# Matmuls of zeros, whose results nobody reads, in four idle stretches of TensorE at the start of an attention, Fourier mixing and MLP kernel

## The chip, the cores and the metric

The kernel runs on one core of one Trainium2 chip. The metric is the device time of one execution in microseconds (us); lower is better. A core has five engines that each work through their own list of instructions in order: PE (TensorE, the matmuls; its weight loads are listed apart as PEld), DVE (VectorE), ACT (ScalarE), POOL (GpSimd) and SP (SyncE, which here issues the DMAs). They meet only at semaphores.

## The reference, cut to what matters

Shapes: batch 8, 8 heads, 576 tokens, head width 64, 32 memory slots, model width 512, hidden width 2048.

```python
a = softmax(phi, over the 32 slots)                       # pooling weights, (8, 8, 576, 32)
k_m, v_m = einsum('bhsm,bhsd->bhmd', a, k), einsum(same, a, v)
attn_out = softmax(q @ k_m.T / 8) @ v_m
x = attn_out with heads side by side                      # (8, 576, 512)
u = x + real(fft(fft(x, axis=1), axis=2))
un = (u - mean(u)) / sqrt(var(u) + 1e-6)                  # over the last axis
out = u + relu(un @ w_ch1) @ w_ch2                        # (512 -> 2048 -> 512)
```

The two weights arrive as 64 bit floating point numbers.

## The kernel before, in words

The tokens are worked off in 36 tiles of 128. A generator called background makes tiles of u for one batch after another; the main loop takes two finished tiles at a time (a chunk, 18 in all), normalises them and runs the two MLP matmuls over eight slices of the hidden width, while background makes the tiles that come next.

The change lies in the head, everything before the first chunk's MLP. For batch 0 it runs so, and the names are those of the profile:

- SP issues the loads in a fixed list: phi (phs), four pairs of heads (k, v and q of a pair in rawt, stg and twice in w2s), the Fourier tables ct and vt, a mask mk (in small), and the first three slices of both weights (w1t, w2s, stg).
- pooling_weights: PE transposes phi (pf and pl, L292), DVE takes the maxima (L293 to L297), ACT the exponentials (L301, L302) and the scaling (L311), PE transposes back (pt_e, L314, and pl, L317), and DVE and ACT copy the result to et (L315, L318).
- pair_memory, for the four pairs: k and v are pooled by f32 matmuls with 64 moving columns (pm, issued at L255; each f32 matmul leaves two records, so 80 in all), and DVE masks what comes out (L346, L347; these need mk).
- pair_scores, for the four pairs: q times the pooled k (psc, also L255, 48 records of the same shape), then the softmax over the slots, mostly on DVE (L440 to L480) with the exponential on ACT (L450).
- values and spectrum: the Fourier transforms by matmul (pv L521, pa L540 and L548) and transposes (pt_vbd, pt_attnT, L246).
- mix_m, mix_x and add_mix: pp_t and px_t on PE, then u in uring on DVE (L603, L617).
- norm_chunk(0): statistics on DVE (L631 to L640), a power on POOL (L641), un on DVE (L642); then PE transposes un (pt_unT, L657) and ACT copies it to unring (L658).
- Then the first chunk's MLP in f32, slice by slice (ph L675, po L692), with the conversion of each weight slice from 64 to 32 bits: ACT L771 and L793, DVE L773, L774 and L784 (and L779 with POOL L782 for some slices). The sum of squares of a slice goes through PE as as_sq (L214). The conversion of the first slice of w1 needs nothing but its load, and stands early on DVE.

From the second chunk on the matmuls are f16 (ph L255 and po L728), which is the long steady part.

The order of each engine's list isn't the order of the code. The program is given to a scheduler that places every instruction by its own forecast of when it can run, and the lists that it makes are then fixed. A forecast that changes in one place can so exchange neighbours on other engines too.

PSUM has 8 banks here: four of pool psg (tag g), two of ps1, two of ps2 (tag o, which the MLP's sums po use later). uring is a ring of eight tiles of 128x512 f32, and its slot 7 is first written by the eighth tile of u.

Of the kernel before, what the change touches and what calls it, by code (L numbers as in the profile page):

```python
# [10 lines left out]
F32 = mybir.dt.float32  # L11
F16 = mybir.dt.float16
# [26 lines left out]
NU = 8  # L39
NHS = 7  # L40
STEPS = 2
NX = 2
GATE1 = [[]] + [["un1", "uh0"]] * 7
GATE2 = [["un1", "uh0"]] * 8
# [87 lines left out]
def kernel(  # L132
# [42 lines left out]
    ident = small[:, 768:832].bitcast(F16)  # L175
    make_identity(nc, ident)
    identf = const.tile([P, P], F32, name="identf")
    make_identity(nc, identf)
# [5 lines left out]
    unring = const.tile([P, 2, 2, CH, NK, P], F16, name="unring")  # L184
    uring = const.tile([P, NU, DM], F32, name="uring")
    hring = const.tile([P, NW, 2, 4, P], F16, name="hring")
# [29 lines left out]

    qi = [0]

    def norm_scale(dst_s, dst_i, sq, n, expo, key):
# [12 lines left out]
        )  # L232
        nc.vector.reciprocal(out=dst_s, in_=dst_i)

    def transpose(dst, src, on_pe, key):
# [13 lines left out]
    def groups():  # L249
# [3 lines left out]
        def mm(out, lhsT, rhs, start, stop):  # L253
            with tc.issue_after(last[0].ins) if start and last[0] is not None else nullcontext():
                m = nc.tensor.matmul(out, lhsT=lhsT, rhs=rhs, start=start, stop=stop)  # L255
            if stop:
                last[0] = m

# [24 lines left out]
    def pooling_weights(b):  # L283
# [4 lines left out]
        for g in range(2):  # L288
            pf.append(psg.tile([P, 512], F32, tag="g", name=f"pf_{b}_{g}"))
            for t in range(NST):  # L290
                dst = pf[g][:, t * P : (t + 1) * P] if t < 4 else pl[:, g * P : (g + 1) * P]
                nc.tensor.transpose(dst, phs[:, t, 2 * g : 2 * g + 2].rearrange("p g c -> p (g c)"), identf)  # L292
            nc.vector.tensor_reduce(out=mx[:, g : g + 1], in_=pf[g], axis=AX.X, op=ALU.max)  # L293
        rest = pl[:, : 2 * P].rearrange("p (g s) -> p g s", g=2)[:, :, : S - 4 * P]
        nc.vector.tensor_reduce(out=mx[:, 2:4], in_=rest, axis=AX.X, op=ALU.max)
        nc.vector.tensor_tensor(out=mx[:, 0:2], in0=mx[:, 0:2], in1=mx[:, 2:4], op=ALU.max)
        nc.vector.tensor_scalar(out=mx[:, 0:2], in0=mx[:, 0:2], scalar1=-1.0, scalar2=None, op0=ALU.mult)  # L297
        su = tiny("su", 4, 2)
        for g in range(2):
# [8 lines left out]
        for g in range(2):  # L308
            r = su[:, 2 + g : 3 + g]
            if b < NX:  # L310
# [5 lines left out]
                half_t = pl[0 : S - 4 * P, (2 + g) * P : (3 + g) * P]  # L316
                nc.tensor.transpose(half_t, pht[:, g, 4 * P :], identf)  # L317
                nc.scalar.copy(out=et32[0 : S - 4 * P, g, 4], in_=half_t)  # L318
# [595 lines left out]

    load_phi(0)
    first = [load_pair(0, 0)]
    nc.sync.dma_start(out=mk, in_=mk_d)
# [33 lines left out]
    while made < 2:  # L951
        made, room = next(bg)
    unTs = {0: norm_chunk(0)}
    hs = {c: [] for c in range(n_chunks)}
# [107 lines left out]
```

## Time and profile before

| what | us |
| --- | --- |
| median of 3 runs | 996.77 (996.4 to 997.15) |
| the profiled execution, its own time | 996.51 |
| the profiled execution, from its first to its last instruction (span) | 994.6 |
| PE busy in the span | 955.8 |
| DVE busy in the span | 568.1 |
| PE busy in the first 50 us | 34.1 |
| PE's longest idle stretches in the first 70 us, by the timeline of PE | 0 to 4.26, 7.40 to 13.43, 44.2 to 48.7, 59.97 to 65.26 |

Some 1.9 us of the execution lie around the span. A row of the timeline gives the start, the duration, the engine, the line, the operation and the tiles (what is written, then what is read), the shape and the number of instructions merged into it; in brackets stands how long the engine had been idle and what ended that. A row of the table of stretches gives, for each engine, its busy time and its number of instructions, then the granted clock of TensorE as a share of full speed, the share of the DMA engines' time and their rate. A row of the chain of waits gives a start, a time, and the work that the end of the program hung on in that time.

### The profile page before, as it was taken

How to read it: one execution, taken by the hardware profiler on the slowest of the kernel's cores; microseconds unless marked ns; L12 is line 12 of the kernel's file. 1: busy time of each engine (PE TensorE's matmuls, PEld its weight loads, DVE VectorE, ACT ScalarE, POOL GpSimd, SP SyncE). 2: the span in 40 equal slices, each digit the busy share in tenths (PEclk: the TensorE clock that was granted, in tenths of full speed). 3: DMA queues.
4: the chain of work that ended last, by engine and by line, in shares of the span. 5: the costliest groups of instructions: out<-in, count | busy, mean ns of one | idle time of the engine just before them, and what ended most of it. 6: DMA issues, size and time to landing. Idle time of an engine off the chain costs nothing.

```text
span 994.6 us, 18638 instructions
## 1 busy us (share of the span) xinstructions
PE 955.8 (96%) x7644; PEld 685.8 (69%) x7644; DVE 568.1 (57%) x1287; ACT 456.3 (46%) x913; POOL 228.0 (23%) x249
## 2 busy tenths in 40 slices
PE   5769999899999999999999999999999999999998
PEld 5756678666677777767767767777777777766664
DVE  1689967867655575657532576657745676311111
ACT  2265557586535563655431555456545543411100
POOL 1122235235221241233120032113311241300000
PEclk9979999999999999999999999999999999999999
DMA  9706545064222641384210643164213411210000
GB/s 351 270 1 253 184 152 154 2 138 117 64 43 59 136 98 41 56 153 103 58 22 22 117 120 61 48 119 121 68 43 62 101 19 35 44 39 4 22 22 22
DMA packets 115957, 88.06 MB, mean 89 GB/s; under 512 B 100384, under 2 KB 100384, under 8 KB 113824
## 3 DMA queue, kind: packets, MB, share of 16 engines
q1 hardware_dynamic: 115872, 86.87, 34.6%
q8 instruction: 60, 0.98, 0.4%
q14 instruction: 25, 0.20, 0.1%
HBM read 58.15 MB, written 9.44 MB: 68 GB/s over the span
## 4 chain that ended last, share of the span: by engine, by line
PE 84%; DVE 9%; ACT 2%; DMA 2%; issue 1%; SPq 0%; POOL 0%; DVEq 0%; ACTq 0%; POOLq 0%
PE po L728 34%; PE ph L255 33%; PE pm L255 5%; PE pp_t L255 3%; PE psc L255 2%; PE px_t L255 1%; PE pa L548 1%; PE pv L521 1%; PE po L692 1%; DVE w1t L784 1%; DVE uring L617 1%; DVE w2s L774 1%; DMA et<-elt 1%; DMA uring<-in_w 1%; DMA rawt<-in_raw 1%
## 5 line engine op out<-in xcount | busy, mean ns | idle before, releaser
L255 PE MATMUL ph<-unring,w1t 128*128 128x256 f16 x3264 | 390.3, 273 | 2.4 <-DVE scratch L638 1.4
L728 PE MATMUL po<-w2s,hring 128*128 128x512 f16 x1632 | 381.1, 380 | 3.1 <-ACT w2s L838 1.8
L255 PEld LDWEIGHTS <-w1t 128*128 128x128 f16 x3264 | 316.0, 98 | 66.3 <-issue 2.6
L728 PEld LDWEIGHTS <-hring 128*128 128x128 f16 x1632 | 157.6, 98 | 161.5 <-issue 5.6
L719 DVE SCALAR_TENSOR_TENSOR hring<-ph,hring 128x512 f16<-128x512 f32 x136 | 93.3, 686 | 157.4 <-ACT hring L718 156.9
L718 ACT ACTIVATE hring<-ph 128x512 f16<-128x512 f32 x136 | 80.1, 589 | 167.7 <-PE ph L255 167.6
L456 POOL TENSOR_TENSOR aring<-aring,scratch 128x384 f32<-128x384 f32 x28 | 24.7, 882 | 186.6 <-DVE scratch L454 163.5
L641 POOL TENSOR_TENSOR scratch<-scratch,small 128x1 f32<-128x1 f32 x36 | 23.9, 679 | 165.6 <-DVE scratch L640 152.9
L255 PEld LDWEIGHTS <-stg 128*128 128x128 f16 x1152 | 46.1, 98 | 10.3 <-issue 1.7
L373 POOL TENSOR_TENSOR stg<-rawt,stg 128x640 f16<-128x640 f32 x12 | 17.6, 1464 | 122.4 <-ACT rawt L372 122.4
L662 POOL TENSOR_TENSOR ud<-un,ud 128x1024 f16<-128x1024 f32 x17 | 36.7, 2160 | 33.9 <-ACT ud L661 33.8
L255 PE MATMUL pm<-et,stg 128*128 128x64 f16 (+1 forms) x780 | 39.1, 203 | 2.0 <-DMA et<-elt 2.0
L440 DVE TENSOR_REDUCE scratch<-psc 128x12 f32<-128x384 f32 x32 | 17.8, 556 | 39.2 <-PE psc L255 39.1
L255 PE MATMUL pp_t<-vh,at 128*128 128x255 f16 (+3 forms) x288 | 36.7, 273 | 0.0
L603 DVE SCALAR_TENSOR_TENSOR share<-pp_t,scratch,small 128x257 f32<-128x257 f32 (+1 forms) x48 | 21.0, 479 | 26.6 <-ACT small L600 26.5
L740 DVE SCALAR_TENSOR_TENSOR uring<-po,small,uring 128x512 f32<-128x512 f32 x34 | 24.5, 744 | 19.2 <-PE po L728 19.2
L675 PE MATMUL ph<-unring,w1t 128*128 128x256 f32 x128 | 33.5, 409 | 2.0 <-DVE w1t L784 1.5
L475 ACT CAST aeo<-eo 128x384 f16<-128x384 f32 x30 | 15.3, 510 | 43.9 <-DVE eo L472 43.9
L450 ACT ACTIVATE aring<-aring,scratch 128x384 f32<-128x384 f32 x24 | 14.6, 610 | 45.0 <-DVE aring L449 45.0
L617 DVE SCALAR_TENSOR_TENSOR uring<-px_t,scratch,share 128x256 f32<-128x256 f32 (+1 forms) x80 | 33.9, 476 | 0.2
L692 PE MATMUL po<-w2s,hring 128*128 128x512 f32 x64 | 31.5, 621 | 2.4 <-ACT hring L678 2.4
L675 PEld LDWEIGHTS ph<-unring,w1t 128*128 128x128 f32 x128 | 26.0, 207 | 11.1 <-issue 4.6
(226 smaller groups left out, 1271.9 us busy)
## 6 DMA issues: line engine op xcount, KB each, us to landing
rawt<-in_raw SPq DMA_DIRECT2D x15, 640.0 KB, 5.6
stg<-in_raw SPq DMA_DIRECT2D x15, 640.0 KB, 5.1
out<-uring SPq DMA_DIRECT2D x36, 256.0 KB, 2.1
stg<-in_w SPq DMA_DIRECT2D x7, 1024.0 KB, 5.1
rawt<-in_raw SPq DMA_DIRECT2D x15, 384.0 KB, 3.2
stg<-in_raw SPq DMA_DIRECT2D x15, 384.0 KB, 3.2
phs<-in_raw SPq DMA_DIRECT2D x32, 160.0 KB, 5.2
w2s<-in_w SPq DMA_DIRECT2D x4, 1024.0 KB, 9.6
```

Source lines behind the costliest of these rows:

```text
L255: m = nc.tensor.matmul(out, lhsT=lhsT, rhs=rhs, start=start, stop=stop)
L456: eng.tensor_tensor(out=a, in0=a, in1=sm.unsqueeze(2).to_broadcast([P, 12, M]), op=ALU.mult)
L603: nc.vector.scalar_tensor_tensor(out=tm[rows, w * NJ : (w + 1) * NJ], in0=pp[rows, :NJ], scalar=beta[rows], in1=qs[rows], op0=ALU.mult, op ...
L617: nc.vector.scalar_tensor_tensor(out=u[rows, hs], in0=px[rows, hs], scalar=igx[rows], in1=tm[rows, w * NJ + half : w * NJ + half + 256], o ...
L641: nc.gpsimd.tensor_tensor(out=rs, in0=rs, in1=half, op=ALU.pow)
L662: marks[f"ul{c}"] = nc.gpsimd.tensor_tensor(out=ud[:, 1], in0=un, in1=ud[:, 0], op=ALU.subtract)
L675: nc.tensor.matmul(ph, lhsT=w[:, k, f * P : (f + 1) * P], rhs=unTs[0][:, k], start=(k == 0), stop=(k == NK - 1))
L692: nc.tensor.matmul(po[t], lhsT=h[:, f, t], rhs=w[:, f], start=(j == 0 and f == 0), stop=(j == NW - 1 and f == UB - 1),)
L718: nc.scalar.activation(h[:, 0], phv, AF.Relu)
L719: nc.vector.scalar_tensor_tensor(out=h[:, 1], in0=phv, scalar=0.0, in1=h[:, 0], op0=ALU.max, op1=ALU.subtract)
L728: nc.tensor.matmul(po[t], lhsT=hs[j][:, lh, f * 2 + t], rhs=w2s[:, j * UB + f, lw, :], start=(j == 0 and f == 0 and i == 0), stop=(j == NW ...
L740: nc.vector.scalar_tensor_tensor(out=u, in0=po[t], scalar=cout if c else 0.5, in1=u, op0=ALU.mult, op1=ALU.add)
```

## The change

A block of 128x512 f16 zeros is made once, by a memset on DVE, in the memory of uring's slot 7. A new function keep_busy(n) issues n matmuls that read this block both as weights (its first 128 columns) and as moving operand (all 512), and write a PSUM tile of the pool ps2 that nothing reads. Each call is placed behind the last matmul or transpose that had been marked so far. Seven counts stand in a table; four are above zero:

- KEEP[0] = 8, right after the loads of phi, ahead of all other work of PE;
- KEEP[1] = 26, after the first transposes of phi and the maxima, ahead of pt_e;
- KEEP[6] = 3, after the second pt_e, ahead of the first pm;
- KEEP[4] = 22, after px_t of the first two tiles, ahead of pt_unT.

That is 59 matmuls of 128x512 f16. No load and no instruction with a result is added or taken away.

```diff
+KEEP = [8, 26, 0, 0, 22, 0, 3]
...
+    uring = const.tile([P, NU, DM], F32, name="uring")
+    zeros = uring[:, NU - 1].bitcast(F16)[:, :DM]
+    nc.vector.memset(zeros, 0.0)
...
+    def keep_busy(n):
+        pt = ps2.tile([P, 512], F32, tag="o", name=f"keep_{len(kept)}")
+        kept.append(pt)
+        with tc.issue_after(marks["pe"].ins) if "pe" in marks else nullcontext():
+            for _ in range(n):
+                nc.tensor.matmul(pt, lhsT=zeros[:, :P], rhs=zeros, start=True, stop=True)
...
             if stop:
-                last[0] = m
+                last[0] = marks["pe"] = m
...
+        if b == 0:
+            keep_busy(KEEP[1])
         su = tiny("su", 4, 2)
...
-                nc.tensor.transpose(half_t, pht[:, g, 4 * P :], identf)
+                marks["pe"] = nc.tensor.transpose(half_t, pht[:, g, 4 * P :], identf)
+                if b == 0:
+                    keep_busy(KEEP[5 + g])
...
     load_phi(0)
+    keep_busy(KEEP[0])
...
     while made < 2:
         made, room = next(bg)
+    keep_busy(KEEP[4])
     unTs = {0: norm_chunk(0)}
```

What this does to the engines' lists is shown at three places. The first is PE from the second group of phi's transposes to the first pooling matmul. Before:

```order
L292 MATMUL pf_1_135<-identf,phs 128x128 x4
L292 MATMUL pl_127<-identf,phs 128x128
L314 MATMUL pt_e_0_153<-identf,phs 128x128 x4
L317 MATMUL pl_127<-identf,phs 64x128
L314 MATMUL pt_e_1_162<-identf,phs 128x128 x4
L317 MATMUL pl_127<-identf,phs 64x128
L255 MATMUL pm_0_170<-et,rawt 128x64 x10
```

Now (rows of the zeros that only repeat are left out; they read uring and write keep):

```order
L304 MATMUL pf_1_145<-identf,phs 128x128 x4
L304 MATMUL pl_137<-identf,phs 128x128
L245 LDWEIGHTS uring
L245 MATMUL keep_155<-uring 128x512
...
L328 MATMUL pt_e_0_190<-identf,phs 128x128 x4
L331 MATMUL pl_137<-identf,phs 64x128
L328 MATMUL pt_e_1_200<-identf,phs 128x128 x4
L331 MATMUL pl_137<-identf,phs 64x128
L245 LDWEIGHTS uring
L245 MATMUL keep_207<-uring 128x512
...
L267 MATMUL pm_0_212<-et,rawt 128x64 x10
```

Twenty-six pairs stand between the transposes and pt_e, and three between the last pl and pm; the rest of PE's list is as it was down to the last psc. (L245 is the added line; the lines behind it are some 12 to 18 higher than before.)

The second place is DVE between the last maskings of pm and the softmax of the first pairs. Before:

```order
L347 TENSOR_TENSOR vmf<-pm_1_183,small 128x128
L773 TENSOR_SCALAR w1t<-w1t 128x1024
L774 SCALAR_TENSOR_TENSOR w1t<-w1t 128x1024
L784 SCALAR_TENSOR_TENSOR w1t<-w1t 128x1024
L346 TENSOR_TENSOR share<-pm_2_196,small 128x64
L347 TENSOR_TENSOR vmf<-pm_2_196,small 128x128
L346 TENSOR_TENSOR share<-pm_3_209,small 128x64
L347 TENSOR_TENSOR vmf<-pm_3_209,small 128x128
L440 TENSOR_REDUCE scratch<-psc_0_222 128x12
L449 TENSOR_TENSOR aring<-psc_0_222,scratch 128x384
L452 TENSOR_REDUCE scratch<-aring 128x12
```

Now:

```order
L363 TENSOR_TENSOR vmf<-pm_1_225,small 128x128
L362 TENSOR_TENSOR share<-pm_2_238,small 128x64
L363 TENSOR_TENSOR vmf<-pm_2_238,small 128x128
L362 TENSOR_TENSOR share<-pm_3_251,small 128x64
L363 TENSOR_TENSOR vmf<-pm_3_251,small 128x128
L789 TENSOR_SCALAR w1t<-w1t 128x1024
L790 SCALAR_TENSOR_TENSOR w1t<-w1t 128x1024
L456 TENSOR_REDUCE scratch<-psc_0_264 128x12
L800 SCALAR_TENSOR_TENSOR w1t<-w1t 128x1024
L456 TENSOR_REDUCE scratch<-psc_1_288 128x12
L465 TENSOR_TENSOR aring<-psc_0_264,scratch 128x384
```

The three steps that convert the first slice of w1 stood between the second and the third pair's masking; now two of them stand behind the fourth pair's and the third behind the first reduction of the scores. Behind these rows the softmax of the four pairs and the values' steps are interleaved differently, with the same operations. On SP the load of mk and that of the first slice of w1 have exchanged places, so mk now goes first.

The third place is PE ahead of the transposes of the first normalised tiles. Before:

```order
L255 MATMUL px_t_441<-vbdt,attnT 128x128
L255 LDWEIGHTS attnT
L255 MATMUL px_t_452<-vbdt,attnT 128x128
L255 LDWEIGHTS attnT
L657 MATMUL pt_unT_468<-identf,un 128x128 x4
L657 MATMUL pt_unT_479<-identf,un 128x128 x4
```

Now:

```order
L267 LDWEIGHTS attnT
L267 MATMUL px_t_494<-vbdt,attnT 128x128
L245 LDWEIGHTS uring
L245 MATMUL keep_505<-uring 128x512
...
L673 MATMUL pt_unT_533<-identf,un 128x128 x4
L673 MATMUL pt_unT_544<-identf,un 128x128 x4
```

Twenty-two pairs stand between px_t and pt_unT. Behind this place neighbours have changed places here and there up to the end of the first chunk; from the third batch on every list is as it was.

More of the change, by code (lines that the diff above doesn't have):

```diff
@@ L184 @@
     unring = const.tile([P, 2, 2, CH, NK, P], F16, name="unring")
-    uring = const.tile([P, NU, DM], F32, name="uring")
     hring = const.tile([P, NW, 2, 4, P], F16, name="hring")
@@ L217 @@
     qi = [0]
+    kept = []
     def norm_scale(dst_s, dst_i, sq, n, expo, key):
@@ L291, in pooling_weights @@
                 dst = pf[g][:, t * P : (t + 1) * P] if t < 4 else pl[:, g * P : (g + 1) * P]
-                nc.tensor.transpose(dst, phs[:, t, 2 * g : 2 * g + 2].rearrange("p g c -> p (g c)"), identf)
+                marks["pe"] = nc.tensor.transpose(dst, phs[:, t, 2 * g : 2 * g + 2].rearrange("p g c -> p (g c)"), identf)
             nc.vector.tensor_reduce(out=mx[:, g : g + 1], in_=pf[g], axis=AX.X, op=ALU.max)
```

## The prediction

> **What bounds the kernel now.** I began with the page's head and its slices of the span, to see where PE isn't full.
>
> ```profile
> span 994.6 us, 18638 instructions
> PE 955.8 (96%) x7644; PEld 685.8 (69%) x7644; DVE 568.1 (57%) x1287; ACT 456.3 (46%) x913; POOL 228.0 (23%) x249
> PE   5769999899999999999999999999999999999998
> PEclk9979999999999999999999999999999999999999
> ```
>
> PE sets the pace from the third slice on; only the head, the first two slices, has holes. What is won there is kept if the part behind is a plain queue for PE. So I next asked for stretches: the head piece by piece, a piece of the next batch, and the steady part.
>
> ```profile
> 7.40:13.40 6.00, 0.00 (x1) 0.00 (x0) 1.54 (x7) 4.12 (x11) 0.00 (x0) 1.00 1.02 412
> 15.60:43.00 27.40, 27.40 (x130) 27.24 (x128) 12.29 (x32) 5.01 (x9) 1.47 (x2) 1.00 1.01 378
> 48.70:52.30 3.60, 3.58 (x23) 2.04 (x25) 3.60 (x11) 1.48 (x4) 1.77 (x3) 1.00 0.00 0
> 59.90:65.20 5.30, 0.07 (x2) 0.00 (x0) 4.60 (x14) 0.00 (x0) 1.17 (x2) 0.75 0.00 0
> 65.20:72.80 7.60, 7.08 (x22) 6.04 (x23) 6.11 (x10) 6.14 (x7) 1.83 (x1) 0.50 0.00 1
> 72.80:94.10 21.30, 20.83 (x114) 14.67 (x112) 21.30 (x31) 11.96 (x21) 3.32 (x2) 1.00 0.53 205
> 147.80:151.30 3.50, 3.50 (x34) 3.50 (x33) 2.81 (x7) 0.71 (x2) 0.67 (x1) 1.00 0.67 150
> 209.00:995.00 786.00, 780.81 (x6574) 547.39 (x6573) 415.94 (x940) 345.09 (x704) 171.81 (x189) 1.00 0.31 67
> ```
>
> The columns are PE, PEld, DVE, ACT, POOL, then the granted clock and the DMA share. Three limits follow one another: PE alone from 15.6 to 43.0 (27.40 of 27.40 us, DVE under half), DVE alone from 72.8 to 94.1 (21.30 of 21.30), PE from 209 on (780.81 of 786). Zeros in PE's holes (7.4 to 13.4, 59.9 to 65.2) can pay only through the clock, and the clock column seems to leave little: it shows 0.50 from about 62.5 to 72.7 and 1.00 before that. That 1.00 is what I doubted. A column of shares can't say whether a stretch without a record was at full speed; the duration of one shape can. The groups of PE, shapes apart, in the first 60 us and from 128 to 158 us:
>
> ```profile
> L255 PE MATMUL pm<-et,w2s 128*128 128x64 f32 x40 | 8.7, 421 | 0.0
> L255 PE MATMUL pm<-et,stg 128*128 128x64 f32 x40 | 4.8, 275 | 0.0
> ```
>
> After the bar stand busy us, the mean ns of one, and idle us. One shape takes 421 ns in batch 0 and 275 in batch 1. In the chain of waits it is the pace, not only the latency, that differs:
>
> ```profile
> 13.43 1.12 PE pt_e L314 x4
> 15.83 16.96 PE pm L255 x80
> 32.79 5.13 PE psc L255 x24
> 124.54 0.66 PE pt_e L314 x4
> 138.98 1.28 PE psc L255 x12
> 148.92 2.23 PE pm L255 x20
> 233.93 2.16 PE po L728 x10
> ```
>
> pm runs at 16.96/80 = 0.212 us a record in the head and 2.23/20 = 0.1115 later; psc at 5.13/24 = 0.214 against 1.28/12 = 0.107. A factor of 1.9 to 2.0 is a clock at half. And the timeline of PE shows when it ended:
>
> ```profile
> 50.48 0.94 PE L548 MATMUL pa<-ct,aeo 128*128 128x145 f16 x6
> 54.26 0.55 PE L548 MATMUL pa<-ct,aeo 128*128 128x145 f16 x6
> 67.88 6.11 PE L675 MATMUL ph<-unring,w1t 128*128 128x256 f32 x16 [0.46 <-ACT unring L658]
> 80.36 3.67 PE L675 MATMUL ph<-unring,w1t 128*128 128x256 f32 x16
> ```
>
> So I read PE as at half clock from the start to about 52 us, and again to 72.7. It stayed so through 27 us of unbroken work, while wide matmuls raised it soon: f16 around 50 us, and ph in the second dip. The narrow ones are held by their weight loads (27.24 of 27.40 busy): at the half clock 64 columns take 0.212 us and 256 take 6.11/16 = 0.382, four times the columns in 1.8 times the time, so the array streams at most half the time. That is too little to raise the clock. Is it enough to keep it? The stretch 147.8 to 151.3 says so: 34 records, nearly all pm and psc, PEld full, and 1.00 throughout.
>
> **The change part by part.** The price of a zero is 2.16/10 = 0.216 us, since po is f16 of 128x512 too, and by the factor of two 0.43 at half clock.
>
> KEEP[0]: eight at half clock are 3.5 us, in a hole of 4.26; the memset ahead of them is one DVE instruction of 128x256, under 0.7 us by the reduction of twice as many elements at 35.39 below. Cost: between 0 and 0.2 us; I take nothing.
>
> KEEP[1]: the hole it lies in, from the timeline of PE:
>
> ```profile
> 4.26 1.09 PE L292 MATMUL pf<-identf,phs 128*128 128x128 f32 x4 [4.26 <-POOL small L195]
> 6.98 0.42 PE L292 MATMUL pl<-identf,phs 128*128 128x128 f32 x1
> 13.43 1.12 PE L314 MATMUL pt_e<-identf,phs 128*128 128x128 f32 x4 [6.03 <-ACT phs L311]
> ```
>
> 26 zeros take 5.6 us at full clock in 6.03, so they are hidden by ACT's exponentials if the clock is up by about 8.2 us; each us later costs 0.5 us, and a clock that never rises costs 26 x 0.43 - 6.03 = 5.1. In front of 7.4 us PE has then worked for some 6 of 7 us, more than the stretch around 50 us that raised it, so I expect the rise between 4 and 11 us: 0 to 1.4 us late, and if pf and pl come faster, 0.4 early. I take 0. KEEP[6]: three are 0.65 us, while pt_e shortens from 1.12 to 0.66 twice; between ACT's two scalings and the copies of et the two cancel. pm starts where it did.
>
> Then the gain. pm: 80 x (0.212 - 0.1115) = 8.0 us. The first pair's psc: 12 x 0.107 = 1.3. The other three pairs' scores come out faster than DVE takes them, and give nothing more. The first scores are ready 9.3 us earlier, at 26.1 in place of 35.4. Who takes them is DVE, and its order has changed:
>
> ```profile
> 21.06 0.23 DVE L346 TENSOR_TENSOR share<-pm,small 128x64 f32<-128x64 f32 x1 [4.71 <-DMA small<-in_mk]
> 24.63 0.68 DVE L773 TENSOR_SCALAR w1t<-w1t 128x1024 int32<-128x1024 int32 x1
> 25.35 1.23 DVE L774 SCALAR_TENSOR_TENSOR w1t<-w1t 128x1024 int32<-128x1024 int32 x1
> 26.61 1.22 DVE L784 SCALAR_TENSOR_TENSOR w1t<-w1t 128x1024 uint32<-128x1024 uint32 x1
> 35.39 0.56 DVE L440 TENSOR_REDUCE scratch<-psc 128x12 f32<-128x384 f32 x1 [2.14 <-PE psc L255]
> 37.12 0.55 DVE L452 TENSOR_REDUCE scratch<-aring 128x12 f32<-128x384 f32 x1 [0.59 <-ACT aring L450]
> ```
>
> The mask lands by 21 us, before the second pair's pm is over, and its load goes one place earlier: no new wait. The conversion of w1 used to fill a hole of DVE; now there is none. The fourth pm ends at 15.8 + 8.9 = 24.7, its masking at 25.1, the two conversions (0.7 + 1.25) at 27.1: the first reduction is 1.0 us late, and the third conversion puts 1.2 us ahead of the second. Loss 2.2. Against it, other pairs' reductions now stand in the wait of 0.59 for ACT: gain 0.5. From there to un DVE and ACT do the same work, so un comes 9.3 - 2.2 + 0.5 = 7.6 us earlier.
>
> Next come the last matmuls ahead of un, by PE's timeline:
>
> ```profile
> 57.32 1.48 PE L255 MATMUL pp_t<-vh,at 128*128 128x257 f16 x12
> 58.63 1.34 PE L255 MATMUL px_t<-vbdt,attnT 128*128 128x128 f16 x16
> ```
>
> In between PE idles after psc as it did, for want of DVE, and the clock falls again. Whether it is back by pp_t depends on how densely pv and pa come; before, it was back at 52. If it isn't, pp_t and px_t take up to 1.48 + 1.34 us more, and the zeros of KEEP[4] start slow. At full clock 22 are 4.75 us in the 5.3 us hole that DVE's statistics leave; with half of them slow they end 1 us late. I bound this by 0 and +3.7 us and take +0.4. Behind the zeros:
>
> ```profile
> 65.26 1.94 PE L657 MATMUL pt_unT<-identf,un 128*128 128x128 f32 x8 [5.29 <-DVE un L642]
> 67.24 0.59 ACT L658 COPY unring<-pt_unT 128x512 f32<-128x512 f32 x1 [0.21 <-PE pt_unT L657]
> 67.72 1.12 ACT L771 ACTIVATE w2s<-w2s 128x1024 f32<-128x1024 f32 x1
> 72.91 1.13 ACT L803 ACTIVATE w1t<-w1t,small 128x1024 f16<-128x1024 f32 x1
> ```
>
> With the clock kept, pt_unT halves and ACT's second copy comes 0.8 us earlier. ph saves 2.4 us (6.11 to 3.67), but ACT has L771 to L803 to do until 74 us whatever PE does, and DVE is full after that: nothing more.
>
> [...]
>
> Sum: -7.6 - 0.8 + 0.4 = -8.0 us. The profiled execution took 996.51, 0.26 below the median of 996.77, so the forecast is 988.5 against the first and 988.7 against the median. Behind the head DVE's full stretch and then PE's move as a whole.
>
> **The rivals.** First, the clock rises and falls back within pm and psc: a longer unbroken run of narrow matmuls than the 3.5 us that were seen at 1.00. Half way through, 4.7 us of the 9.3 are won, and the conversion again lies partly in DVE's waits: 991.5 to 993.
>
> Second, zeros don't raise the clock: no row shows a matmul of zeros. Then KEEP[1] ends at 7.4 + 11.1 = 18.5 and pt_e starts 5.1 us late, KEEP[6] adds 1.3, and PE's narrow run, still at half clock, sets the scores 6.4 us later; KEEP[4] lies behind real work that raised the clock at 52 and fits. 996.5 + 6.4 = 1002.9. It ends slower only if the clock is still low through pm; a rise by 11 us costs but 1.4. For it: nothing but the missing row. Against it: the engine works through the same instruction.
>
> Third, the 421 ns aren't the clock: the DMA engines are full from 15.6 to 43.0 (1.01), and their writes might slow the weight loads. Then only KEEP[4] pays: 996.5 - 0.8 = 995.7. Against it stand six pa in 0.94 us at 50 us with a DMA share of 0.00 (48.7 to 52.3), and in 0.55 four us later.
>
> Fourth, the gain is made and lost again up to 209 us, by exchanged neighbours or by loads: near 996. The loads for later slices are issued when DVE frees their room and move with it, which speaks against it.
>
> **How the numbers follow.** Forecast 0.75; rivals 0.09, 0.06, 0.05, 0.05. The likeliest case's own range: early by 0.4, no loss in the tail and the two conversions better hidden (-3) give 985.5; 1.4 late at KEEP[1] and 3.7 in the tail give 993.8. Some 0.72 lies in there; with the first rival, up to 994.5, it is 0.8. About 0.2%, 2 us, is what a measurement of this kernel tells from no change. Faster: 0.75 + 0.09 = 0.84. Same: 0.05 + 0.05 = 0.10. Slower: 0.06.
>
> **What would show it.** Right: pm of batch 0 at 275 ns from its first record, pt_e at 0.66 us for four, the first L440's counterpart near 27 us, un near 57.5, no stretch at 0.50 behind pt_unT, and the 786 us from 209 on unchanged. Wrong: pm at 421; pt_e starting at 18 us; DVE's first reduction early but pt_unT not; or a clock that drops within the narrow run.

## The result, and the profile after

The changed kernel took 990.29 us (median of 3 runs, 988.95 to 991.04) against 996.77 (996.4 to 997.15): a ratio of 0.9933, with a 95% interval of 0.991 to 0.9956. It is faster, and the forecast was 988.7. One thing has to be known from the start: executions of the kernel before fall into two groups some 8 us apart (shown below), and the three that the ratio was taken from all lay in the upper one.

The page of the profile after, its head and the slices of PE and of the granted clock:

```profile
span 988.3 us, 18757 instructions
PE 955.3 (97%) x7703; PEld 675.8 (68%) x7703; DVE 566.7 (57%) x1288; ACT 455.9 (46%) x913; POOL 229.0 (23%) x249
PE   9589998799999999999999999999999999999998
PEclk9689999999999999999999999999999999999999
```

59 matmuls were added and the busy time of PE is 0.5 us lower: what the zeros cost (15.1 us, next view) the real matmuls gave back. The span is 6.3 us shorter. The groups of PE in the first 60 us, shapes apart:

```profile
L245 PE MATMUL keep<-uring 128*128 128x512 f16 x59 | 15.1, 413 | 1.2 <-DVE uring L180 1.2
L267 PE MATMUL pm<-et,w2s 128*128 128x64 f32 x40 | 4.6, 275 | 0.0
L564 PE MATMUL pa<-ct,aeo 128*128 128x145 f16 x24 | 4.0, 328 | 0.0
```

pm takes 275 ns, where it took 421; these 40 of its 80 records take 4.6 us instead of 8.7. Not all went that way: pa (the Fourier step behind the softmax) takes 328 ns a matmul. PE's timeline shows where:

```profile
1.19 3.60 PE L245 MATMUL keep<-uring 128*128 128x512 f16 x8 [1.19 <-DVE uring L180]
4.58 1.06 PE L304 MATMUL pf<-identf,phs 128*128 128x128 f32 x4
6.41 0.71 PE L304 MATMUL pf<-identf,phs 128*128 128x128 f32 x4 [0.56 <-DMA phs<-in_raw]
7.06 5.78 PE L245 MATMUL keep<-uring 128*128 128x512 f16 x26
13.37 0.66 PE L328 MATMUL pt_e<-identf,phs 128*128 128x128 f32 x4 [0.53 <-ACT phs L325]
46.86 0.42 PE L556 MATMUL pa<-ct,aeo 128*128 128x290 f16 x1 [2.89 <-DVE aeo L496]
50.91 1.52 PE L267 MATMUL pp_t<-vh,at 128*128 128x257 f16 x12
53.15 4.91 PE L245 MATMUL keep<-uring 128*128 128x512 f16 x22
58.54 1.25 PE L673 MATMUL pt_unT<-identf,un 128*128 128x128 f32 x8 [0.47 <-DVE un L658]
67.07 5.37 PE L708 MATMUL po<-w2s,hring 128*128 128x512 f32 x8 [2.89 <-ACT hring L694]
```

The first eight zeros take 3.60/8 = 0.45 us each, the next 26 take 5.78/26 = 0.222: the clock rose in between. Between the two groups of pf the same four records shrink from 1.06 to 0.71. pt_e takes 0.66. But pa starts on a PE that idled 2.89 us for DVE and takes 0.42 where 0.28 is its time at full clock, so the clock had gone again. And the last row shows a hole that wasn't there before: ph is now done in 3.72 us instead of 6.11, and po waits for ACT. The table of stretches gives the granted clock for the same places:

```profile
15.30:29.70 14.40, 14.40 (x129) 14.26 (x127) 6.66 (x17) 2.53 (x4) 0.00 (x0) 1.00 1.03 420
30.50:47.80 17.30, 7.41 (x42) 4.02 (x43) 16.30 (x53) 8.48 (x17) 6.66 (x8) 0.50 0.77 260
...
53.20:58.50 5.30, 4.87 (x25) 1.99 (x21) 4.62 (x14) 0.00 (x0) 1.18 (x2) 1.00 0.00 0
67.10:71.40 4.30, 4.30 (x7) 1.76 (x8) 4.30 (x6) 1.13 (x3) 0.00 (x0) 0.61 0.01 4
202.00:988.00 786.00, 780.81 (x6574) 547.37 (x6573) 416.65 (x940) 345.44 (x705) 172.44 (x190) 1.00 0.29 67
```

What was 27.4 us of pure PE (15.6 to 43.0) is now 14.4, at 1.00 throughout although PEld is as full as before. Behind it the clock is at 0.50 from 30.5 us through the Fourier transforms to 51, at full again under the 22 zeros, and at 0.61 on the mean of one piece behind the new hole. The long steady part is the same to 0.01 us: 780.81 busy of 786. The chain of waits:

```profile
15.48 8.89 PE pm L267 x80
24.82 0.61 DVE w1t L789
25.45 1.23 DVE w1t L790
27.15 1.13 DVE w1t L800
57.84 0.56 DVE un L658
```

pm is 8.89 us of it instead of 16.96. Behind pm the chain goes straight to DVE, to the conversion of w1 that now stands in its way.

### The profile page after: what moved, and what is told of

It is laid out like the page before. It is cut to its first block, busy times and chain, and to the rows that moved or that the text cites. A ratio compares the mean times of both kernels' runs of the same rounds, so it can differ in the third digit from the quotient of the medians.

```text
span 988.3 us, 18757 instructions
## 1 busy us (share of the span) xinstructions
PE 955.3 (97%) x7703; PEld 675.8 (68%) x7703; DVE 566.7 (57%) x1288; ACT 455.9 (46%) x913; POOL 229.0 (23%) x249
## 4 chain that ended last, share of the span: by engine, by line
PE 82%; DVE 9%; ACT 4%; DMA 3%; issue 2%; POOL 0%; SPq 0%; DVEq 0%; ACTq 0%
PE po L744 35%; PE ph L267 33%; PE pm L267 4%; PE pp_t L267 3%; PE psc L267 2%; PE px_t L267 1%; PE pa L564 1%; PE pv L537 1%; DVE uring L633 1%; DVE w1t L800 1%; PE po L708 1%; DVE w1t L790 1%; DMA et<-elt 1%; DVE w2s L790 1%; DMA rawt<-in_raw 1%
## 5 line engine op out<-in xcount | busy, mean ns | idle before, releaser
L267 PEld LDWEIGHTS <-stg 128*128 128x128 f16 x1152 | 46.1, 98 | 10.5 <-issue 1.7
L267 PE MATMUL pm<-et,stg 128*128 128x64 f16 (+1 forms) x780 | 37.0, 199 | 2.1 <-DMA et<-elt 2.1
L496 DVE SCALAR_TENSOR_TENSOR aeo<-aeo,small,eo 128x128 f16<-128x128 f16 x30 | 25.9, 864 | 12.0 <-ACT aeo L491 11.9
L480 POOL TENSOR_TENSOR ahring<-aring,ahring 128x320 f16<-128x320 f32 x29 | 24.9, 858 | 33.3 <-ACT ahring L479 33.2
```

Source lines behind the costliest of these rows:

```text
L480: nc.gpsimd.tensor_tensor(out=ahl[:, :, 64:128], in0=av[:, 0:5], in1=ahl[:, :, 0:64], op=ALU.subtract)
L496: marks[f"s{b}_{g}"] = nc.vector.scalar_tensor_tensor(out=av4[:, 1, :, 0, gs], in0=av4[:, 0, :, 0, gs], scalar=mk[:, 64:65], in1=eo[:, :, ...
```

## The experiments

All were compared with runs of the kernel before on the same chip, taken beside them. First the main numbers in one place; "first reduction" is DVE's first reduction of the scores, pt_unT the transposes of the first normalised tiles, both as start times in the profiled execution, and the groups of before are told apart below.

| kernel | first reduction | pt_unT | span | time of all executions, median (range) |
| --- | --- | --- | --- | --- |
| before, upper group (shown first) | 35.39 | 65.26 | 994.6 | 996.51 (995.26 to 999.01), 58 of 82 |
| before, lower group (a later profile) | 26.77 | 56.31 | 986.8 | 988.37 (986.2 to 989.76), 24 of 82 |
| the change | 26.59 | 58.54 | 988.3 | 990.29 (988.95 to 991.04), n 3 |
| the change, run again | 26.68 | 58.75 | 988.6 | 989.86 (989.47 to 990.51), n 12 |
| zeros at the head alone | 26.29 | 58.22 | 992.8 | 993.84 (992.74 to 994.82), n 10 |
| zeros behind px_t alone | 35.19 | 65.06 | 998.3 | 1000.16 (990.85 to 1001.25), n 10 |
| none between pf and pt_e | 26.88 | 58.76 | 990.2 | 994.02 (991.62 to 1005.38), n 10 |
| zeros on 32 rows | 42.77 | 72.85 | 1004.7 | 1006.27 (1004.46 to 1006.72), n 4 |
| zeros through the whole front | 26.33 | 57.51 | 986.4 | 988.76 (987.23 to 990.56), n 12 |
| the same, run again on another chip | 26.58 | 57.76 | 985.9 | 988.01 (986.52 to 990.1), n 6 |
| the whole front, and w1's conversion forward | 25.16 | 60.92 | 989.7 | 991.4 (989.8 to 993.38), n 12 |
| the whole front without those behind px_t | 26.90 | 58.07 | 992.9 | 993.78 (992.54 to 995.6), n 12 |
| the whole front with fewer ahead of pm | 25.49 | 57.69 | 987.5 | 989.46 (987.58 to 990.28), n 6 |

### One end of the change at a time

```diff
-KEEP = [8, 26, 0, 0, 22, 0, 3]
+KEEP = [8, 26, 0, 0, 0, 0, 3]
```

> Only the zeros of the first 15 us stay (8, 26 and 3); the 22 ahead of pt_unT are gone. Theory (the gain is the clock of pm and psc, 9.3 us of PE of which DVE passes on some 6.7): pm of batch 0 stays at 275 ns, un comes at 57.8 us as with the change, the clock falls in the hole of 5.3 us and pt_unT and ph run at half speed, which costs 0.7 us and then nothing, since ACT and DVE are full: 990.3 + 0.7 = 991.0 us. Rival (the clock kept at pt_unT is a main part, since ph is 2.4 us shorter): 993 or more.

The head does what it does in the change (first reduction 26.29, pt_unT 58.22), yet the whole takes 993.84, a ratio of 0.9987 (0.9963 to 1.0011). That is the rival's number, but not for its reason: the first po starts only 0.3 us later than in the change (67.38 against 67.07). The rest was lost far behind the zeros: set beside the same matmuls of the change, those of this run are 2.2 us late by 134 us and 4.6 from 240 on. One of the rows that hold it, from the waits of PE between 80 and 245 us, which stands at 1.8 us in the same view of the change:

```profile
PE ph L267 <- DVE hring L735: 3.8, 2, 2.1
```

Columns: total us, times, longest. It isn't the lists alone. Behind two of its stalls the clock stood at 0.50 for a whole window (97.1 to 100.5 and 127.8 to 131.2 us), where the change has 1.00. So 22 matmuls of zeros more or less reorder the lists of other engines, and the stalls that come of it, with the clock that falls behind some of them, move 3 to 4 us.

```diff
-KEEP = [8, 26, 0, 0, 22, 0, 3]
+KEEP = [0, 0, 0, 0, 22, 0, 0]
```

> Only the 22 zeros ahead of pt_unT stay. Theory: pm of batch 0 at 421 ns as before, un where it was (64.6 us), pt_unT and ph at full speed: 0.7 us gained, 996.0 us, no difference that can be measured. Rival (kept clock at pt_unT is a main part): 994 or less.

Eight of ten executions took 998.35 to 1001.25, two 990.85 and 991.64: two groups again, as in the kernel before. In the profiled one pm is at 421 ns, as before, and the 22 zeros do their own work, by PE's timeline:

```profile
65.06 1.24 PE L673 MATMUL pt_unT<-identf,un 128*128 128x128 f32 x8 [0.54 <-DVE un L658]
```

1.24 us in place of 1.94: 0.7 us. With a start that was 0.2 us earlier all along, these transposes end 0.9 us earlier than before (66.3 against 67.2), and the first po starts 0.9 earlier too. What followed lost it and more: the matmuls from 140 to 160 us stand level with those of before, and from 240 us on they are 3.7 us late. Most of that is in one row of the waits, which before doesn't have:

```profile
PE ph L267 <- DMA unring<-ud: 3.1, 1, 3.1
```

The term of the tail is real and under 1 us; lists that fell out another way buried it.

### What the 26 zeros are for

```diff
-KEEP = [8, 26, 0, 0, 22, 0, 3]
+KEEP = [8, 0, 0, 0, 22, 0, 3]
```

> The 26 zeros between the first transposes and pt_e are gone; the 8 ahead of them, the 3 ahead of pm and the 22 ahead of pt_unT stay. Theory (the clock must be up when the narrow matmuls begin, and an idle stretch of 6 us lets it fall; narrow matmuls can't raise it): the clock rises at 4 to 8 us and falls again by 14, pm at 421 ns, the time as with the 22 alone, 996 us. Rival (once raised, the clock stays up over a hole of 6 us, or the 3 zeros and pt_e bring it back): pm at 275 ns and 990.3 us.

My theory missed here. I had thought that without the 26 the clock would fall in the hole ahead of pt_e and pm would be slow. It did fall, but it was back at once:

```profile
12.81 1.11 PE L328 MATMUL pt_e<-identf,phs 128*128 128x128 f32 x4 [6.13 <-ACT phs L325]
14.99 1.49 PE L245 MATMUL keep<-uring 128*128 128x512 f16 x3
16.27 2.40 PE L267 MATMUL pm<-et,rawt 128*128 128x64 f32 x20
```

pt_e at half clock (1.11) and three slow zeros filled the time up to 16.4 us, and pm ran 2.40/20 = 0.12 us a record. In two of ten executions it seems to have gone otherwise: 1003.97 and 1005.38, while the other eight took 991.62 to 995.46. The two have no timeline, but their mean granted clock is 0.971 against 0.981 to 0.986 in the eight, which over some 1000 us is 20 to 30 us more at half clock, about the length of pm and psc there. Behind the head (from 58 us on) this kernel's lists are those of the run with only the 22, with the same stalls. What lies between these two profiles is the clock under pm and psc, the order of the softmax steps in the head, and one window at 0.50 near 180 us that this run was spared: 6.3 us from 100 to 170 us, and a span of 990.2 against 998.3 at the end.

### Zeros on a quarter of the array

```diff
-                nc.tensor.matmul(pt, lhsT=zeros[:, :P], rhs=zeros, start=True, stop=True)
+                nc.tensor.matmul(pt, lhsT=zeros[0:32, :P], rhs=zeros[0:32], start=True, stop=True)
```

> All 59 zeros stay, but each is a matmul of 32 rows (a quarter of the array's rows) by 128 columns, still 512 moving columns. Theory A (what raises the clock is how long the array streams): like the change, pm at 275 ns, 990.3 us, up to 1 us either way for the lists, which the scheduler makes a little different. Theory B (what counts is how much of the array works): the clock stays at half until real work raises it, each zero takes 0.43 us, pt_e starts 5 us late at 18.5, and the time is 6 us above before: 1003 us.

These stream the same 512 columns without a gap, but occupy 32 of the array's 128 rows. The clock stayed down until 61 us (pm took 421 ns). PE's timeline, and two stretches behind px_t (PE, PEld, DVE, ACT, POOL, clock, DMA share, rate):

```profile
7.93 11.27 PE L245 MATMUL keep<-uring 32*128 32x512 f16 x26
```

```profile
68.00:71.30 3.30, 3.30 (x17) 1.43 (x16) 3.30 (x11) 0.00 (x0) 0.00 (x0) 1.00 0.00 0
71.40:81.00 9.60, 9.14 (x27) 6.82 (x26) 7.25 (x11) 6.73 (x8) 3.54 (x3) 0.50 0.00 1
```

26 take 11.27 us, 0.43 each: they neither raise the clock, nor keep it where it was up. From 68.0 to 71.3 PE was busy all the time with nothing else, and behind that stands 0.50. What the clock follows here is not busy time (3.30 of 3.30 us). The ratio was 1.0126 (1.0075 to 1.0176); the price of zeros that don't raise the clock is thus +7.4 us at the first reduction and about +10 at the end, though the lists differ from before's from 204 us on.

### The change again, and zeros wherever the front idles

> The changed kernel itself, as the base for the others of this call and to see its spread beside that of before. Theory (the zeros make certain what before reaches only now and then, a full clock in pm): medians near 990.3 us, all executions within 2 us of it, while before has a few executions near 988 among many near 996.4. Rival (the fast executions of before come from elsewhere): the changed kernel shows a second group some 8 us lower too.

On this chip the change took 989.86 us, all twelve executions within 1.04 us, and the kernel before 995.7 at the median, but in two groups: 15 executions from 995.7 to 998.12 and 14 from 986.62 to 988.92. So the ratio came out at 0.9986 (0.9959 to 1.0013). Same kernels, another mixture.

The next kernel adds 41 zeros to the change where its PE idled between the scores and pa:

```diff
+MID = [12, 14, 12]
...
+            if b == 0:
+                keep_busy(3)
+            vsum = all_sum(vq[:, 0:1], 1, f"vq_{b}")
+            if b == 0:
+                keep_busy(MID[0])
...
             ks = slice(kb * P, kb * P + P)
+            if b == 0:
+                keep_busy(MID[1 + kb])
```

> The change, and 41 more zeros: 3 behind the last psc, 12 behind the sum that follows it (as_vq), 14 ahead of the first pa and 12 ahead of the third, so that the clock stays up from the first zeros to pt_unT. The lists behind the head are those of before here. Theory (pa, attnT and pv at half clock cost 1.6 us between the last of DVE's aeo and un, and the changed lists behind the head cost some more): un at 56.2 in place of 57.8 us, 988.0 us. Rival (DVE alone sets un, the half clock there is hidden; lists behind the head don't matter): 990.3 us. Zeros that stand in the way of pv and pa would show as a later un: 991 or more.

It took 988.76 us, 1.1 below the change on the same chip. The clock holds through the whole front:

```profile
4.00:30.00 26.00, 24.72 (x182) 19.61 (x180) 10.80 (x27) 8.36 (x20) 0.51 (x3) 1.00 1.01 395
30.00:50.00 20.00, 15.38 (x115) 8.16 (x115) 17.23 (x55) 10.77 (x22) 6.22 (x8) 1.00 0.74 240
50.00:66.00 16.00, 11.87 (x72) 7.68 (x71) 12.44 (x25) 9.73 (x15) 3.90 (x3) 1.00 0.01 2
```

What that is worth is read from DVE: the last aeo (the input of pa) and un, in this kernel, in the change and in the kernel before:

```profile
45.76 0.75 DVE L497 SCALAR_TENSOR_TENSOR aeo<-aeo,small,eo 128x128 f16<-128x128 f16 x1
56.82 1.16 DVE L666 TENSOR_SCALAR un<-uring,scratch 128x512 f32<-128x512 f32 x2 [0.61 <-POOL scratch L665]
```

```profile
46.04 0.76 DVE L496 SCALAR_TENSOR_TENSOR aeo<-aeo,small,eo 128x128 f16<-128x128 f16 x1
```

```profile
54.26 0.86 DVE L480 SCALAR_TENSOR_TENSOR aeo<-aeo,small,eo 128x128 f16<-128x128 f16 x1 [0.18 <-ACT aeo L475]
64.57 1.16 DVE L642 TENSOR_SCALAR un<-uring,scratch 128x512 f32<-128x512 f32 x2 [0.61 <-POOL scratch L641]
```

From the end of the last aeo to un it takes 56.82 - 46.51 = 10.31 us here, 57.84 - 46.80 = 11.04 in the change (un stands in its chain of waits above) and 64.57 - 55.12 = 9.45 before. The clock is worth 0.7 of it. The other 0.9 is left when both stand at full clock there, so it comes from the lists. The rows between show where, first of DVE and PE in this kernel, then of DVE in the kernel before, whose pp_t and px_t the prediction shows (57.32 and 58.63):

```profile
49.28 0.86 DVE L584 SCALAR_TENSOR_TENSOR at<-pa,at 128x290 f16<-128x290 f32 x2 [2.77 <-ACT at L583]
49.84 1.05 PE L268 MATMUL pp_t<-vh,at 128*128 128x257 f16 x8 [0.25 <-DVE at L584]
```

```profile
56.24 1.22 DVE L560 SCALAR_TENSOR_TENSOR at<-pa,at 128x290 f16<-128x290 f32 x3
```

The same 14 records of pa lie behind the last aeo in both, and pp_t begins 2.20 us behind its end in both (48.71 and 57.32). But in this kernel, as in the change, ten of the transposes pt_attnT stand ahead of the last eight pa on PE, and ACT copies their result before it takes the last two parts of pa. So DVE's last at ends 3.6 us behind the last aeo instead of 2.3, and pp_t waits for it: pp_t and px_t take 3.50 us instead of 2.65. In the change, where pa and the transposes run at half clock, pp_t begins 4.11 us behind the last aeo and then shows no wait. No run moved that order by itself.

### Moving the conversion of w1

The kernel with zeros through the whole front, and the conversion of w1's first slice made ahead of the fourth pair's masking on DVE:

```diff
                     mem[g] = pair_memory(b, g, first[g], vmf, ivs)
+                    if g == 2:
+                        to_f32(parts_w1[0], w1_f32(0), "1_0", True)
```

(The later call for that slice then only sums the squares, and the fourth pair's two maskings are issued after the conversion.)

> As the run before, and the conversion of w1's first slice is ordered ahead of the fourth pair's masking, where DVE had holes of 1.8 us. Theory (two of the three conversions stood in the way of the first reduction of the scores, and cost what the prediction put at 2.2 us): un 1.0 us earlier than in the run before, 987.0 us, give or take 1.5 for the lists behind the head, which differ again. Rival (DVE waits for the scores there, so that nothing is won): no earlier un.

The conversion did what it should: the first reduction starts at 25.16 instead of 26.33. But the scheduler drew another list, and pt_unT came 3.4 us later, not earlier. The row of PE that shows it, first from this kernel, then from the one above:

```profile
38.20 0.40 PE L259 MATMUL pt_vbd<-small,share 128*128 128x128 f16 x4 [4.24 <-ACT share L533]
```

```profile
33.49 0.40 PE L259 MATMUL pt_vbd<-small,share 128*128 128x128 f16 x4 [0.44 <-ACT share L532]
```

The scaling of the values on ACT (share), which needs a sum that DVE finishes, comes 4.7 us later, and the transforms with it. The clock then fell too (0.50 from 39.3 to 46.1 us), so that the 14 zeros ahead of pa took 4.50 us instead of 3.19; how much of the 3.4 is theirs was not separated. 991.4 us: a miss of my 987.0.

### Why the kernel before has two times

> The kernel before, unchanged, profiled once more, because its executions have fallen into two groups near 996.4 and 988.2 us. Theory (the grid of the clock's 3.41 us windows has another phase in each execution; in some of them the transposes pt_e and the first of pm fill a whole window, and the clock rises before pm): an execution near 988 shows pm at about 275 ns from some 17 us on, a clock record of 1.0 near 17 us, the first reduction of the scores near 26.5 us and pt_unT near 58; an execution near 996 shows pm at 421 ns and the first record near 52. Rival (the two groups part elsewhere, by the loads or by the steady part): an execution near 988 shows pm at 421 ns and the first reduction near 35.4 all the same.

> The same kernel as in the look before, for a second execution; the theory and its rival expect the same of it: near 988 us with pm at 275 ns and the first reduction near 26.5, or near 996 us with pm at 421 ns and the first reduction near 35.4; by the rival the two are not tied to each other.

Two more profiled executions are one of each kind: 995.94 us and 988.72. The groups of PE in the first:

```profile
L255 PE MATMUL pm<-et,w2s 128*128 128x64 f32 x40 | 8.7, 421 | 0.0
```

and in the second, with PE's timeline and DVE's first reduction:

```profile
L255 PE MATMUL pm<-et,w2s 128*128 128x64 f32 x40 | 4.6, 275 | 0.0
```

```profile
13.43 1.11 PE L314 MATMUL pt_e<-identf,phs 128*128 128x128 f32 x4 [6.03 <-ACT phs L311]
15.61 3.08 PE L255 MATMUL pm<-et,rawt 128*128 128x64 f32 x20
18.53 2.40 PE L255 MATMUL pm<-et,stg 128*128 128x64 f32 x20
```

```profile
26.77 0.56 DVE L440 TENSOR_REDUCE scratch<-psc 128x12 f32<-128x384 f32 x1 [0.92 <-PE psc L255]
```

The same program, no zeros, and pm speeds up in its first twenty records: 3.08 us, then 2.40. Here is the whole gain of the change's head without the change: first reduction 26.77, pt_unT 8.7 us earlier than in the first of the two (64.98), span 986.8 against 993.9. It also is the best measure of what the clock under pm and psc is worth at equal lists: 7.1 us at the end.

Why one execution and not the other? In the traces the clock changes in steps of a grid of 3.41 us (at 52.26, 62.50 and 72.74 in the execution shown first, three steps apart; at 6.60, 30.49, 50.97, 68.04 and 71.45 in the change, seven, six, five and one; at 17.15, 34.22 and 44.46 here, five and three), and the grid lies differently in each of the three. In this execution one of its windows goes from 13.74 to 17.15, filled by pt_e and the first, wide apart records of pm; in the execution shown first the nearest, counted back from 52.26, goes from 14.71 to 18.13 and holds more of pm and less of pt_e. A window missed costs 35 us of half clock here, from 17 to 52. How full these windows were is estimated in the last section: 0.74 to 0.80 in the one that ended at 17.15, 0.66 in the one from 14.71 to 18.13. That the grid's phase decides is read from four profiles (these two, the one shown first, and the run without the 26 zeros), not forced by an experiment; and why the lower group had 2 of 25 executions on one chip and 14 of 29 on another stays open.

### Two more attempts at the front

The kernel with zeros through the whole front, without the 22:

```diff
-KEEP = [8, 26, 0, 0, 22, 0, 3]
+KEEP = [8, 26, 0, 0, 0, 0, 3]
```

> The change with zeros between the scores and pa (as in the run that kept PE busy there), but without the 22 behind px_t. The lists of the two differ in 17 of PE's rows. Theory (the 22 zeros only keep pt_unT and the first ph at the full clock; ph's weights come late and ACT holds the slice anyway): pt_unT at 1.97 instead of 1.25 us at worst, end 0 to 0.8 us later than with them, so 988.8 to 989.6. Rival (the first slices need the clock, 16 ph and 8 po at half of it before it rises again): 2 to 4 us later, 991 to 993.

993.78 us: outside both ranges, for a reason that neither named. pt_unT is only 0.6 us later, and at the last po of the fourth slice it is 0.8 behind (100.05 against 99.27). Then the waits of PE from 84 to 145 us, here and with the 22:

```profile
PE po L716 <- POOL w2s L806: 5.3, 1, 5.3
```

```profile
PE po L716 <- POOL w2s L806: 2.0, 1, 2.0
```

On DVE, steps of the next tiles now stand between the conversions of w2's slices, so one slice is ready 3 us later. The lists again, and the clock behind them: after the longer wait it stands at 0.50 for two windows (107.8 to 114.7 us) where it was one (107.4 to 110.8), and from 115 us on the run is 5.1 us behind. The wait is 3.3 of the 4.3 that are lost here, the rest can be the second window.

The same kernel with the 22, and fewer zeros ahead of pm:

```diff
-KEEP = [8, 26, 0, 0, 22, 0, 3]
+KEEP = [0, 14, 0, 0, 22, 0, 0]
```

> The kernel that kept PE busy through the whole front, with fewer zeros ahead of pm: none before pf, 14 instead of 26 behind it, none between pt_e and pm (the 41 in the middle and the 22 behind px_t stay). The scheduler now puts DVE's first reduction of the scores between the first and the second step of the conversion of w1's first slice; behind the head the lists are those of the run with more zeros. Theory (14 zeros at half clock stand from about 7.1 to 13.0 us, so one whole window of 3.41 us ends in them or in the transposes behind them, in every phase): the clock rises between 10.4 and 13.9 us in every execution, pm at 275 ns, no second group; first reduction near 25.2 instead of 26.3, pt_unT near 56.5 instead of 57.5, end 987.0 to 988.8. Rival (fewer zeros leave it to the phase again): some executions 8 us longer than the others, near 996. Rival on the lists: the reduction moved forward sends the work behind it another way, as it did where the conversion itself was ordered forward; pt_unT later than 58 and the end at 990 to 992.

> The kernel that kept PE busy through the whole front (8, 26 and 3 zeros ahead of pm, 3, 12, 14 and 12 in the middle, 22 behind px_t), once more beside the one with fewer zeros. Theory: one group of executions, 987.2 to 990.6, median near 988.8 as before; its median lies about 1 us below that of the change as it was made (989.9). Rival (that difference was the chip's): median at 989.9 or above.

On one chip: 989.46 us with fewer, 988.01 (986.52 to 990.1, n 6) with all, and 995.76 before (10 of 11 executions in the upper group), ratios of 0.9935 (0.9911 to 0.996) and 0.9925 (0.9902 to 0.9948). Fourteen zeros are enough for the clock: in the profile it is up at 9.1 us, and no execution of six is in an upper group. The expected head start isn't there at pt_unT:

```profile
25.49 0.56 DVE L457 TENSOR_REDUCE scratch<-psc 128x12 f32<-128x384 f32 x1 [0.32 <-PE psc L268]
57.69 1.18 PE L681 MATMUL pt_unT<-identf,un 128*128 128x128 f32 x8 [0.55 <-DVE un L666]
```

Against the run with all the zeros beside it (26.58 and 57.76) the reduction is 1.1 us earlier and pt_unT level. In between the clock fell for one window (0.50 from 36.4 to 39.8 us; the eight pv at 36.62 take 1.92 us in place of 1.05), and DVE's list differs too; which of the two took the head start isn't shown. With all the zeros the front held its 988.8 and 988.0 on two chips; it is the best version here, 1.1 us below the change, and about level with the lower group of the kernel before.

## Why the prediction was right, point by point

**The reading of the half clock** held. In every profile with pm at 421 ns the clock's first rise comes behind psc, in every one with 275 it comes ahead of pm or within its first twenty records, and the DMA engines are as full in both (1.01 before, 1.03 after). The third rival, DMA traffic as the cause, falls with that; so does the second, since zeros do raise the clock, and its price of +6.4 at the scores was measured as +7.4 with the zeros that don't. The first, a fall within pm and psc, wasn't seen in any profile: 14 us of narrow matmuls stay at 1.00. "Too little to raise the clock, enough to keep it" is right for these matmuls by themselves. What the prediction didn't see is that pt_e together with the first of them is at the edge: 24 of 82 executions of the kernel before lie in the lower group, whose profile shows the full clock under pm without any zeros. It took one profiled execution, and three times that happened to agree, for the kernel. So the reading is right for the upper group, and that the ratio of the result shows it is in part luck: with 58 of 82 in the upper group, three in a row come about every third time, and against the mixture of a later run the same change came out at 0.9986 (0.9959 to 1.0013).

**KEEP[0], KEEP[1], KEEP[6] at nothing**: right. The clock rose at 6.6 us, pm starts at 15.32 instead of 15.62. (The memset took 0.27 us. The reduction that bounded it reads 384 elements against 256, not twice as many; the bound holds all the same.)

**The scores**: predicted 9.3 us earlier at PE, and the first reduction at 27.1. Measured 26.59, 8.8 earlier. pm ended at 24.4 instead of 24.7, and each step of masking and conversion began 0.1 to 0.2 us ahead of the end of the one before.

**From the first reduction to the last aeo**: predicted +0.7 (1.2 for the third conversion, less 0.5), measured 20.21 against 19.73 us, +0.5.

**The tail** is the step that was mis-sized. I named the risk (the clock falls behind psc; is it back by pp_t?), bounded it by 0 and 3.7, and took 0.4. It measured 11.04 - 9.45 = +1.6. The bound priced pp_t and px_t, which came at 1.52 and 1.06 us against 1.48 and 1.34, so they lost nothing; what ran slow were pa and the transposes ahead of them, 4.11 us from the last aeo to pp_t instead of 2.20, and these had no price. By the kernel that kept the clock up, 0.7 of the 1.6 is won with the clock, and 0.9 stays because of the order of pt_attnT and pa, which I hadn't seen in the lists. So un came 6.7 us earlier; the text had -7.6 and +0.4, so -7.2. The bound itself was added up wrongly as well: 22 zeros with half of them slow take 7.1 us, which is 1.8 over the hole of 5.3 and not 1. They took 4.91, at full clock. The range was laid about the forecast loosely too: its upper end adds 3.7 to a sum that already holds 0.4 of it, and its lower end starts from 988.5.

**pt_unT and ACT's copy**: predicted -0.8. From pt_unT's start (-6.7) to the first po (-7.4) another 0.7 came.

**Behind**: predicted that DVE's full stretch and PE move as a whole. They moved as a whole from about 200 us on, but at -6.4 there (the first ten po in a row start at 206.48 instead of 212.93) and -6.3 at the end. About 1 us of the -7.4 went to other neighbours in the lists, a little of the fourth rival. Elsewhere it was more than a little: in the experiments the lists of kernels that differ in a few zeros, with the clock that falls behind their stalls, cost 3 to 5 us. That this change lost only 1 was luck that the trace of before couldn't tell.

**The clock behind pt_unT**: the text had no stretch at 0.50 there. One of 3.4 us came, at 68 us, because the faster ph left PE waiting for ACT. That ph's 2.4 us would be worth nothing was right, and the hole of 2.89 is where they went.

In sum: -8.8 + 0.5 + 1.6 - 0.7 + 1.1 = -6.3 of span, against a forecast of -8.0.

## What to carry to other kernels

Check the clock by the duration of one shape in two places before a column of shares is believed (pm at 421 and 275 ns here, both under a column of 1.00), and profile more than one execution before a difference of a per cent is given a cause: this kernel had two times, 988.37 and 996.51 us, and by its profiles what parted them was where the clock's grid lay. Zeros in idle stretches made the full clock under pm certain here (all twelve executions of the change, run again, lay within 1.04 us); give them the whole array (on 32 rows they cost 1.26% and raised nothing), put them ahead of the first long run of narrow matmuls, and count on losing part of the gain where the clock falls again (0.50 from 30.5 to 51 us in the change). Where a scheduler draws the lists, an added instruction can reshuffle engines far away, so of several placements with the same effect on the clock in the head the lists behind it decide, and they have to be measured.

## What the runs showed of the hardware

Matmuls over 32 of 128 rows, streaming without a gap, neither raised the clock nor kept it (0.50 behind 3.3 us of nothing else), while f32 matmuls of 64 columns over all rows, busy by the records but held by their weight loads (PEld 27.24 of 27.40 us before), kept it for 13 us (1.00 from 17.10 to 30.50 in the lower group's profile) and didn't raise it in 27 (pm and psc at 421 ns before, from 15.6 to 43.0). What the clock follows can be estimated from the records. At half clock a window of 3.41 us has room for 8 zeros of 0.43 us, that is 8 x 512 = 4096 columns, and at full clock (0.216 us for the same shape) for twice that. An f32 record costs twice its columns: po takes 0.46 us in f32 (3.68 us for 8, at 142.75 before) and 0.22 in f16, for 512 columns each. A record that uses a part of the array is counted by that part, an assumption that here only the zeros on 32 rows bear out.

- pm alone at half clock: 16 records of 0.212 us, 16 x 128 = 2048 of 4096 columns, 0.50. It never raised the clock.
- pm alone at full clock: 30 records of 0.1115 us, 30 x 128 of 8192 columns, 0.47. It kept the clock.
- The window from 13.74 to 17.15 in the lower group's profile: 1.87 us of transposes that stream without a gap (0.21 us for 128 f32 columns), and pm in the other 1.54: about 0.55 + 0.23 = 0.78, or 0.74 to 0.80 record by record. The clock rose.
- The window from 14.71 to 18.13 in the execution shown first: 0.90 us of transposes, the rest pm, 0.66 record by record. The clock stayed.
- Zeros on 32 rows, a full window of them: 0.25. The clock fell.
- The window from 27.08 to 30.49 in the change, the last of psc and then next to nothing: 0.34. The clock fell.

Counted so over the fourteen profiles, no window below 0.7 raised the clock and every one above 0.81 did; at full clock every one below 0.29 lost it and none above 0.41 did. In between both happened. This is an estimate, with some 150 windows at half clock behind it, not a rule that was tested.

The transposes pt_e count for the clock here. In the lower group's profile the window from 13.74 to 17.15 holds them and the first of pm, and the clock is up behind it; pm alone never raised it in 27 us. So the transposes, 1.87 of the 3.41 us there, must have helped.

What surprised me is how sharp the two groups are. Nothing lies between 989.76 and 995.26 us in 82 executions of the kernel before, and what parts them is, by these profiles, decided within one window of 3.41 us near 15 us, in an execution of a thousand.
